# Attention into a routed expert layer: row stores on GpSimd's queue, loads first in a step, logits two steps after sums, and the early block split during attention

## The chip, the cores and the metric

The kernel runs on one core of a Trainium2 chip. A core has TensorE (PE, matmuls), VectorE (DVE), ScalarE (ACT), GpSimd (POOL) and SyncE (SP, which here only issues DMAs), each with an in-order queue of its own. The metric is the device time of one execution in microseconds; the figure shown is a median of several runs.

## What is computed

The reference is attention with a soft cap on the scores, whose output is fed to a layer of eight experts, one per token.

```python
# q, k, v: 8 batches x 12 heads x 448 tokens x 64
s = scale * (q @ k.T);  s = cap * tanh(s / cap)
a = exp(s - max);  x = (a / sum(a)) @ v            # rows x: 3584 tokens x 768
logits = x @ w_gate                                # 8 experts
e = argmax(logits);  g = softmax(logits)[e]
out[t] = g[t] * (relu(x[t] @ w1[e]) @ w2[e])       # w1: 768 x 1024, w2: 1024 x 768
```

Tokens are sorted by expert, and each expert's tokens are computed in blocks.

## The kernel before

**Attention.** A group of four heads (`m`, 24 of them, three to a batch) has seven tiles of 64 keys. A step `k` (84 of them, `STEPS`) handles two tiles: TensorE makes the scores of tiles 2k and 2k+1 (line 242), ScalarE applies two tanh (line 251) and, for the step before, one exp (line 254), TensorE multiplies the tiles of three steps before with the values (`pv`, line 300), and VectorE adds up the exponentials (`adds`, line 259). The scores have two PSUM buffers, the exponentials `pt` four, and one `m` at a time has its output in PSUM (`po`). So when the first tile of a step is the last of its `m`, the second tile's `pv` is held back to the next step, after `outp` (line 307) has copied the output to `ot`.

**What hangs on a batch.** When the last `m` of batch b is done (step n + 3 in the code), its work is put into the following steps from a table: `at(step, place, function)`, where the places within a step are `act`, `pe0` (before `pv`), `pe1` (after it) and `v` (after `adds`). `sums` makes the denominators, `logits` the gate's products, `rec_v` and `rec_p` the reciprocals, spread over partitions, `rec_c` (line 387) writes them into the last six columns of the row tile `yt`, `log_v` and `log_p` finish the logits, `route_v`, `route_s` and `route_g` find the expert and its weight, `place_p` and `place_v` the slot of each token, `place_d` scatters token numbers to the slots by indirect DMAs of GpSimd (line 503). `turn` (line 318) transposes each output into `yt`, and `store` (line 469) sends a batch's rows, 448 x 4 pieces of 792 bytes, to DRAM in four quarters. The casts of `rec_v` are on GpSimd in all batches but the last.

**SP's queue.** It carries the loads of q, k and v (lines 173 to 176, for the `m` two ahead, issued at the end of a step once the scores of an `m` are done, two buffers), the stores, and, in the second half, `values_load` of the chosen expert's row and the sixteen weight loads of the early block (line 776). All of these are issued in program order, and each waits at the head of the queue until it may go.

**The early block.** After four of eight batches the expert with the most tokens is chosen (`first_block`), and 224 of its tokens, block -2, are gathered (`load_x`, indirect DMAs of GpSimd), scaled (`scale_x`, four steps before the end), transposed by `trans_x` (line 880) and split into a high and a low part by `split_x` (lines 886, 887), so that three matmuls with a shorter type stand for one in float32. The weights are split likewise (`high` on ScalarE, line 791; `low` on VectorE or GpSimd, line 796). In the kernel before, the transposes and splits of block -2 start when the last scores are done, together with the last steps of attention.

**After attention.** TensorE's program order is: `sums` and `logits` of the last batch, `up(-2, 0)` (line 906, 18 matmuls), `up(-2, 1)`, `rec_p`, `up(-2, 2)`, `up(-2, 3)`, `log_p`, and so on, with the last batch's routing threaded between the work of block -2. Block -1, and then the large and small blocks, follow from about 400 us to the end.

The lines around the loop that the change rearranges:

```python
        if not live:
            if k == STEPS:
                split_w1(0, G)
                split_xs(-2, 0, 2)
                split_w1(1, G)
        do(k, "pe0")
```

Of the kernel before, what the change touches and what calls it, by code (L numbers as in the profile page):

```python
# [125 lines left out]
def attention_moe(tc, qT, kT, vL, capd, wgL, w1a, w1b, w2a, w2b, cst, cmk, out):  # L126
# [14 lines left out]
    rpool = pools("rpool", side="right")  # L141
    raw = pools("raw", bufs=2, side="right")
# [9 lines left out]
    raws = {}  # L152

    def load(m, part):

        b, i = divmod(m, NQ)
        p = slice(2 * i, 2 * i + 2)
        if part == 0:
            qr = raw.tile([128, 2, S], F32, name="qr")
            kr = raw.tile([128, 2, S], F32, name="kr")  # L160
            raws[m] = qr, kr, pb.tile([128, KT, 2, D], F32, name="vr", bufs=3)
        qr, kr, vr = raws[m]
        if m == 0:
            if part == 0:
                nc.sync.dma_start(out=kr[:, :, 0:128], in_=kT[b, :, p, 0:128])
                nc.scalar.dma_start(out=qr[:, 0], in_=qT[b, :, 0])
                nc.sync.dma_start(out=qr[:, 1], in_=qT[b, :, 1])
                nc.scalar.dma_start(out=capt, in_=capd)
                nc.sync.dma_start(out=kr[:, :, 128:S], in_=kT[b, :, p, 128:S])
            else:  # L170
                nc.sync.dma_start(out=vr, in_=vL[b, :, i])
        elif part == 0:
            nc.sync.dma_start(out=kr, in_=kT[b, :, p])
            nc.sync.dma_start(out=qr, in_=qT[b, :, p])
        else:
            nc.sync.dma_start(out=vr, in_=vL[b, :, i])
# [85 lines left out]
    def adds(k):  # L262

        t = 2 * k
        m, g = divmod(t, KT)
        pt = pts[k]
        if m % 2 == 0 and g == 0 or m % 2 == 1 and g == 1:
            accs[m] = pb.tile([128, 2, 2, S], F32, name="acc")
            p4s[m] = pb.tile([128, 2, S], F32, name="p4", bufs=4)
        if g == KT - 1:  # L270

            p4 = p4s[m]
            add(p4, accs[m][:, 0], accs[m][:, 1])
            add(p4, p4, pt[:, 0])
        elif m % 2 == 0:
            if g == 2:
                add(accs[m], pts[k - 1], pt)
            elif g == 4:
                add(accs[m], accs[m], pt)
        elif g == 1:  # L280
            add(accs[m][:, 0], pts[k - 1][:, 1], pt[:, 0])
        elif g == 3:
            add(accs[m][:, 1], pts[k - 1][:, 1], pt[:, 1])
            add(accs[m][:, 0], accs[m][:, 0], pt[:, 0])
        else:
            add(accs[m], accs[m], pt)
            add(p4s[m], accs[m][:, 0], accs[m][:, 1])
# [178 lines left out]
    def store(b, quarters=range(4)):  # L466
        xv = xd[4 * b * S : 4 * (b + 1) * S, :].rearrange("(q j a) x -> a j q x", j=32, a=4)
        for a in quarters:
            nc.sync.dma_start(out=xv[a], in_=yts[b][32 * a : 32 * a + 32])
# [49 lines left out]
    def first_block():  # L519
# [10 lines left out]
        for i in range(2):  # L530
# [10 lines left out]
        row = nc.values_load(  # L541
            ti[0:1, 0:1],
# [5 lines left out]
        f0.update(e0=e0, oh=oh, t=t, ti=ti, row=row)  # L548
# [240 lines left out]
    def high(i, f):  # L789
        w, r = ((w1s, w1r), (w2s, w2r))[i - 1]  # L790
        A.copy(out=w[f][0], in_=r[f // 4][:, f % 4, :])
# [6 lines left out]
    def split_w1(f, e=V):  # L798
        high(1, f)
        low(1, f, e)  # L800
# [55 lines left out]
    m = {}  # L856
# [25 lines left out]
    def split_x(j, k, e):  # L882
# [3 lines left out]
        A.copy(out=xh, in_=xt)  # L886
# [105 lines left out]
    for b in range(B - 1):  # L992

        n = (KT * (b * NQ + NQ) - 1) // 2
        at(n + 3, "pe1", sums, b)
        at(n + 4, "pe0", logits, b)
        at(n + 4, "v", turn, b * NP + 4)
        at(n + 4, "v", rec_v, b, G)
        at(n + 5, "v", turn, b * NP + 5)
        at(n + 5, "v", log_v, b)  # L1000
        at(n + 6, "pe1", rec_p, b)
        at(n + 6, "pe1", log_p, b)
        at(n + 7, "v", rec_c, b)
        at(n + 7, "v", route_v, b)
        at(n + 7, "v", store, b, range(0, 2))
        at(n + 8, "act", route_s, b)
        at(n + 8, "pe1", place_p, b)
        at(n + 8, "v", store, b, range(2, 4))
        at(n + 8, "v", route_g, b)
        at(n + 9, "v", place_v, b)  # L1010
        for q in range(4):
            at(n + 10 + q // 2, "v", place_d, b, q)
# [6 lines left out]
    n_first = (KT * B_FIRST * NQ - 1) // 2 + 10  # L1019
    at(0, "v", constants)  # L1020
    at(n_first, "v", first_block)
    for i in range(2 * FC):
        at(n_first + 1 + i + i // 2, "v", load_w0, i)
# [4 lines left out]
    at(STEPS - 4, "v", scale_x, -2)  # L1028

    held = []  # L1030
    for k in range(STEPS + 3):
        live = k < STEPS
        if live:
# [6 lines left out]
        if not live:  # L1040
            if k == STEPS:
                split_w1(0, G)
                split_xs(-2, 0, 2)
                split_w1(1, G)
        do(k, "pe0")
# [13 lines left out]
        if k == STEPS + 1:  # L1059
            split_xs(-2, 2)  # L1060
        do(k, "v")
        for n in range(QUADS - 2):
            if k == (KT * (n + 1) - 1) // 2 + 1:
                load(n + 2, 0)
                load(n + 2, 1)
        if k == STEPS - 1:
            pools.close("raw")
            xp = m["xp"] = pools("xp", side="right", **tw)
            for i in "hl":
                m["x" + i] = xp.tile([128, KC, LARGE], F32R, name="x" + i)  # L1070
            for f in range(2):
                w1s[f] = chunk(xp, f"w1{f}")
            for i in range(XT):
                trans_x(-2, i)
# [11 lines left out]
    b = B - 1  # L1086
    sums(b)
    logits(b)
# [4 lines left out]
    up(-2, 0)  # L1093
# [21 lines left out]
    store(b)  # L1115
# [221 lines left out]
```

## Time and profile before

| | us |
|---|---|
| median of 3 runs | 884.2 (883.1 to 886.51) |
| profiled execution | 883.69 |
| its span, first to last instruction | 881.9 |
| TensorE busy | 813.8 (92%) |
| VectorE busy | 552.4 (63%) |
| ScalarE busy | 473.3 (54%) |
| GpSimd busy | 358.0 (41%) |

Attention takes the span to about 340 us; from 444 us on TensorE hardly pauses. TensorE's matmuls overlap and their ends are modelled, so its busy share is not its load. A group's row gives line, engine, operation, what is written from what, the count, then busy us and mean ns, then the engine's idle time just before and what ended most of it. A row of waits gives the engine and line that waited, for whom, us in total, times, and the longest. A row of the timeline gives start, duration, engine, line, operation, count, and in brackets the idle time before it. SPq is SP's queue of DMA issues.

### The profile page before, as it was taken

To read this page: it belongs to the slowest core of one execution; us is meant where nothing else is said; L and a number is where in the kernel's file an instruction comes from. 1 tells how busy PE (TensorE), PEld (TensorE's weight loads), DVE (VectorE), ACT (ScalarE), POOL (GpSimd) and SP (SyncE) were. 2 spreads that over 40 slices of the span, in tenths; PEclk is the share of its full clock that TensorE was granted. 3 is DMA by queue.
4 is the path that set the end of the run, shared out by engine and by line. 5 is a ranking of instruction groups with operands and counts; after the bars stand their busy time and mean duration, and the time that the engine had idled before them with its cause. 6 is when DMAs were issued, how large, how long until landed. Compare 5 with 4: busy or idle time off the path is not lost. (4 is left out here: it accounts for less than half of the span.)

```text
span 881.9 us, 14403 instructions
## 1 busy us (share of the span) xinstructions
PE 813.8 (92%) x5716; PEld 586.1 (66%) x5716; DVE 552.4 (63%) x944; ACT 473.3 (54%) x556; POOL 358.0 (41%) x333
## 2 busy tenths in 40 slices
PE   8998989897979797798999999999999999999894
PEld 3223333332323333598899999999999999999793
DVE  2677787778667869965664944836638448366620
ACT  7988988897879888332443432423323324234310
POOL 1002120212142203555747067477475673745610
PEclk9999999998999999898999999999999999999997
DMA  6316161618395812042474112451721124444200
GB/s 220 126 64 190 64 191 63 192 67 214 127 237 175 262 64 66 1 98 92 155 302 154 66 38 72 168 201 65 287 87 42 42 73 177 192 172 170 67 34 34
DMA packets 44955, 112.67 MB, mean 128 GB/s; under 512 B 8321, under 2 KB 27203, under 8 KB 41808
## 3 DMA queue, kind: packets, MB, share of 16 engines
q1 hardware_dynamic: 28496, 51.16, 19.3%
q0 software_dynamic: 16096, 60.28, 19.2%
q8 instruction: 47, 0.77, 0.4%
q10 hardware_dynamic: 288, 0.23, 0.1%
q14 instruction: 28, 0.23, 0.1%
HBM read 101.77 MB, written 23.04 MB: 142 GB/s over the span
## 5 line engine op out<-in xcount | busy, mean ns | idle before, releaser
L910 ACT ACTIVATE hb<-ph 128x448 fp32r<-128x448 f32 (+1 forms) x80 | 38.4, 481 | 284.2 <-PE ph L906 279.2
L251 ACT ACTIVATE pt<-sp,qsc 128x896 f32<-128x896 f32 x168 | 161.0, 1015 | 46.0 <-PE po L300 25.2
L242 PE MATMUL sp<-qr,kr 64*64 64x448 f32 x1344 | 152.7, 560 | 26.0 <-DMA qr<-in_qT 21.8
L911 DVE SCALAR_TENSOR_TENSOR hb<-ph,hb 128x448 fp32r<-128x448 f32 (+1 forms) x80 | 43.1, 541 | 186.5 <-ACT hb L910 186.4
L300 PE MATMUL po<-pt,vr 64*64 64x448 f32 x1344 | 149.1, 559 | 3.1 <-DVE ot L307 3.1
L751 POOL DMA_INDIRECT xg<-xd,xi x114 | 129.7, 1138 | 54.7 <-issue 32.6
L254 ACT ACTIVATE pt<-pt,capt 128x1792 f32<-128x1792 f32 x84 | 151.2, 1802 | 0.0
L242 PEld LDWEIGHTS sp<-qr,kr 64*64 64x64 f32 x1344 | 46.2, 135 | 112.4 <-ACT pt L251 55.1
L300 PEld LDWEIGHTS po<-pt,vr 64*64 64x64 f32 x1344 | 57.0, 139 | 82.0 <-issue 75.4
L761 POOL DMA_INDIRECT out<-ys,xi x84 | 90.6, 1078 | 25.6 <-issue 23.2
L503 POOL DMA_INDIRECT ids<-tokg,slots x32 | 38.8, 1214 | 129.8 <-DVE slots L497 122.5
L259 DVE TENSOR_TENSOR acc<-acc,pt 128x1792 f32<-128x1792 f32 (+1 forms) x36 | 61.2, 1700 | 37.9 <-ACT pt L254 37.9
L259 DVE TENSOR_TENSOR acc<-pt 128x896 f32<-128x896 f32 (+1 forms) x36 | 50.2, 1396 | 15.6 <-ACT pt L254 15.5
L370 POOL CAST rb<-rec 96x56 bf16<-96x56 f32 x7 | 6.4, 918 | 130.6 <-DVE rec L362 130.6
L886 ACT CAST xh<-xt 128x448 fp32r<-128x448 f32 (+1 forms) x60 | 28.5, 504 | 40.6 <-DVE xt L880 40.6
L751 POOL DMA_INDIRECT w1r<-in_w1b,widx x8 | 11.1, 1386 | 84.5 <-DVE w17l L796 83.9
L307 DVE COPY ot<-po 128x448 f32<-128x448 f32 x48 | 27.5, 614 | 23.2 <-PE po L300 23.2
L880 DVE STREAM_TRANSPOSE xt<-xg 128x448 f32<-128x448 f32 (+1 forms) x60 | 31.5, 550 | 1.0
L887 DVE TENSOR_TENSOR xl<-xt,xh 128x448 fp32r<-128x448 f32 (+1 forms) x57 | 31.2, 573 | 0.7 <-ACT xh L886 0.5
L870 DVE TENSOR_TENSOR xg<-xg,sc 128x448 f32<-128x448 f32 (+2 forms) x60 | 27.9, 535 | 0.3
L259 DVE TENSOR_TENSOR p<-acc 128x896 f32<-128x896 f32 x24 | 25.8, 1077 | 0.4
L906 PE MATMUL ph<-xl,w10h 128*128 128x448 f32 (+1 forms) x60 | 21.5, 358 | 3.3 <-DVE xl L887 3.1
(353 smaller groups left out, 1922.4 us busy)
## 6 DMA issues: line engine op xcount, KB each, us to landing
vr<-in_vL SPq DMA_DIRECT2D x24, 448.0 KB, 5.8
kr<-in_kT SPq DMA_DIRECT2D x23, 448.0 KB, 5.3
qr<-in_qT SPq DMA_DIRECT2D x23, 448.0 KB, 5.8
xd<-yt SPq DMA_DIRECT2D x20, 346.5 KB, 6.0
xd<-w2r SPq DMA_DIRECT2D x12, 346.5 KB, 6.3
xg<-xd,xi POOLq DMA_INDIRECT x114, 2.7
w1r<-in_w1a SPq DMA_DIRECT2D x4, 384.0 KB, 9.0
w1r<-in_w1b SPq DMA_DIRECT2D x4, 384.0 KB, 6.2
```

What stands on the lines that cost most here:

```text
L242: PE.matmul(sp[w, r, 0:S], kr[h, c, 64 * g : 64 * g + 64], qr[h, c, :], start=True, stop=True)
L251: A.activation(out=pts[t // 2][:, t % 2], in_=sps.pop(t)[:, :, 0:S], func=AF.Tanh, scale=qsc)
L254: A.activation(out=pts[k], in_=pts[k], func=AF.Exp, scale=capt)
L259: V.tensor_tensor(out=o, in0=a, in1=b, op=ALU.add)
L300: PE.matmul(pvs[m][c][w, 0:S], vr[r, g, j, :], pt[r, j, :], start=g == 0, stop=g == KT - 1)
L503: i = G.indirect_dma_start(out=ids, out_offset=bass.IndirectOffsetOnAxis(ap=slots[0:p, c : c + 1].bitcast(U32), axis=0), in_=tokg[0:p, c, ...
L751: G.indirect_dma_start(out=dst, out_offset=None, in_=src, in_offset=bass.IndirectOffsetOnAxis(ap=idx.bitcast(U32), axis=0), bounds_check=b ...
L761: i = G.indirect_dma_start(out=dst, out_offset=bass.IndirectOffsetOnAxis(ap=idx.bitcast(U32), axis=0), in_=src, in_offset=None, bounds_che ...
L880: V.transpose(out=xt.rearrange("p (q j) -> p q j", j=32), in_=xg[:, 0 : n // 32, 32 * k : 32 * k + 32])
L887: e.tensor_tensor(out=m["xl"][:, k, 0:n], in0=xt, in1=xh, op=ALU.subtract)
L910: A.activation(out=hh, in_=ph, func=AF.Relu)
L911: V.scalar_tensor_tensor(out=hl, in0=ph, scalar=0.0, in1=hh, op0=ALU.max, op1=ALU.subtract)
```

## The change

- `store` takes the issuing engine: GpSimd for the first seven batches, all four quarters together one step after `rec_c`, SP for the last.
- The loads of q, k and v are issued at the start of a step, ahead of its scores, and no longer after its `v` work.
- `logits` moves from before `pv` in step n + 4 to after `pv` in step n + 5; all that follows it (`log_v`, `rec_p`, `log_p`, `rec_c`, the routing, `place_*`) comes one step later. `rec_v` goes ahead of `turn`. The choice of the early block and its weight loads come one to three steps later, and `values_load` stands on its own, two steps after the choice.
- `scale_x` of block -2 moves from four steps before the end to eleven; its six transposes and splits go into steps 75 to 82, two at a time, the copies and the subtractions on GpSimd. The first two weight chunks are split on GpSimd alone, in step 83. The buffers for the rows are held from the start.
- The last `fold` (the sum of two halves of the exponentials) is taken after the loop; `up(-2, 0)` is ahead of the last batch's `logits` and `sums`, which change places.

```diff
-            add(p4s[m], accs[m][:, 0], accs[m][:, 1])
+            if m < QUADS - 1:
+                fold(m)
+
+    def fold(m):
+        add(p4s[m], accs[m][:, 0], accs[m][:, 1])
...
-    def store(b, quarters=range(4)):
+    def store(b, e):
...
-        for a in quarters:
-            nc.sync.dma_start(out=xv[a], in_=yts[b][32 * a : 32 * a + 32])
+        for a in range(4):
+            e.dma_start(out=xv[a], in_=yts[b][32 * a : 32 * a + 32])
...
-    def split_x(j, k, e):
+    def split_x(j, k, e, eh=A):
...
-        A.copy(out=xh, in_=xt)
+        (eh.copy if eh is A else eh.tensor_copy)(out=xh, in_=xt)
...
+        d = n + 5
         at(n + 3, "pe1", sums, b)
-        at(n + 4, "pe0", logits, b)
+        at(n + 4, "v", rec_v, b, G)
         at(n + 4, "v", turn, b * NP + 4)
-        at(n + 4, "v", rec_v, b, G)
         at(n + 5, "v", turn, b * NP + 5)
-        at(n + 5, "v", log_v, b)
-        at(n + 6, "pe1", rec_p, b)
-        at(n + 6, "pe1", log_p, b)
-        at(n + 7, "v", rec_c, b)
-        at(n + 7, "v", route_v, b)
-        at(n + 7, "v", store, b, range(0, 2))
-        at(n + 8, "act", route_s, b)
-        at(n + 8, "pe1", place_p, b)
-        at(n + 8, "v", store, b, range(2, 4))
-        at(n + 8, "v", route_g, b)
-        at(n + 9, "v", place_v, b)
+        at(d, "pe1", logits, b)
+        at(d + 1, "v", log_v, b)
+        at(d + 2, "pe1", rec_p, b)
+        at(d + 2, "pe1", log_p, b)
+        at(d + 3, "v", rec_c, b)
+        at(d + 3, "v", route_v, b)
+        at(d + 4, "act", route_s, b)
+        at(d + 4, "pe1", place_p, b)
+        at(d + 4, "v", store, b, G)
+        at(d + 4, "v", route_g, b)
+        at(d + 5, "v", place_v, b)
         for q in range(4):
-            at(n + 10 + q // 2, "v", place_d, b, q)
+            at(d + 6 + q // 2, "v", place_d, b, q)
...
-    n_first = (KT * B_FIRST * NQ - 1) // 2 + 10
+    n_first = (KT * B_FIRST * NQ - 1) // 2 + 11
     at(0, "v", constants)
     at(n_first, "v", first_block)
+    at(n_first + 2, "v", first_row)
     for i in range(2 * FC):
-        at(n_first + 1 + i + i // 2, "v", load_w0, i)
+        at(n_first + 3 + i + i // 2, "v", load_w0, i)
...
-    at(STEPS - 4, "v", scale_x, -2)
+    at(STEPS - 11, "v", scale_x, -2)
+    for k in range(KC):
+        at(STEPS - 9 + k // 2 * 3, "v", trans_x, -2, k)
+        at(STEPS - 8 + k // 2 * 3, "v", split_x, -2, k, G, G)
...
     for k in range(STEPS + 3):
         live = k < STEPS
+        for n in range(QUADS - 2):
+            if k == (KT * (n + 1) - 1) // 2 + 1:
+                load(n + 2, 0)
+                load(n + 2, 1)
...
-            if k == STEPS:
-                split_w1(0, G)
-                split_xs(-2, 0, 2)
-                split_w1(1, G)
-        do(k, "pe0")
...
-        if k == STEPS + 1:
-            split_xs(-2, 2)
         do(k, "v")
-        for n in range(QUADS - 2):
-            if k == (KT * (n + 1) - 1) // 2 + 1:
-                load(n + 2, 0)
-                load(n + 2, 1)
         if k == STEPS - 1:
             pools.close("raw")
-            xp = m["xp"] = pools("xp", side="right", **tw)
...
+            wa = pools("wa", side="right", **tw)
             for f in range(2):
-                w1s[f] = chunk(xp, f"w1{f}")
-            for i in range(XT):
-                trans_x(-2, i)
+                w1s[f] = chunk(wa, f"w1{f}")
+            for f in range(2):
+                split_w1(f, G, G)
+    fold(QUADS - 1)
...
+    up(-2, 0)
+    logits(b)
     sums(b)
-    logits(b)
...
-    up(-2, 0)
```

More of the change, by code (lines that the diff above doesn't have):

```diff
@@ L141, in attention_moe @@
     rpool = pools("rpool", side="right")
+    xp = pools("xp", side="right")
     raw = pools("raw", bufs=2, side="right")
@@ L152, in attention_moe, with load @@
     raws = {}
-    def load(m, part):
-        b, i = divmod(m, NQ)
+    m = {"xp": xp}
+    for i in "hl":
+        m["x" + i] = xp.tile([128, KC, LARGE], F32R, name="x" + i)
+    def load(mq, part):
+        b, i = divmod(mq, NQ)
         p = slice(2 * i, 2 * i + 2)
@@ L160, in load @@
             kr = raw.tile([128, 2, S], F32, name="kr")
-            raws[m] = qr, kr, pb.tile([128, KT, 2, D], F32, name="vr", bufs=3)
-        qr, kr, vr = raws[m]
-        if m == 0:
+            raws[mq] = qr, kr, pb.tile([128, KT, 2, D], F32, name="vr", bufs=3)
+        qr, kr, vr = raws[mq]
+        if mq == 0:
             if part == 0:
@@ L540, in first_block, with first_row @@
         V.tensor_copy(out=ti, in_=t)
-        row = nc.values_load(
-            ti[0:1, 0:1],
+        f0.update(e0=e0, oh=oh, t=t, ti=ti)
+    def first_row():
+        f0["row"] = nc.values_load(
+            f0["ti"][0:1, 0:1],
             engines=[mybir.EngineType.SP],
@@ L547, in first_block @@
         )
-        f0.update(e0=e0, oh=oh, t=t, ti=ti, row=row)
     def second_block():
@@ L787, in chunk, with high @@
         return [pool.tile([128, DM], F32R, name=name + i) for i in "hl"]
-    def high(i, f):
+    def high(i, f, e=A):
         w, r = ((w1s, w1r), (w2s, w2r))[i - 1]
-        A.copy(out=w[f][0], in_=r[f // 4][:, f % 4, :])
+        (e.copy if e is A else e.tensor_copy)(out=w[f][0], in_=r[f // 4][:, f % 4, :])
     def low(i, f, e=V):
@@ L796, in low, with split_w1 @@
         e.tensor_tensor(out=lo, in0=r[f // 4][:, f % 4, :], in1=hi, op=ALU.subtract)
-    def split_w1(f, e=V):
-        high(1, f)
+    def split_w1(f, e=V, eh=A):
+        high(1, f, eh)
         low(1, f, e)
@@ L854, in load_x @@
             gather(xg[:, g, :], xd[0:rows, :], xi[:, g : g + 1], rows - 1)
-    m = {}
     def scale_x(j):
@@ L1039, in attention_moe @@
             expo(k - 1)
-        if not live:
-            if k == STEPS:
-                split_w1(0, G)
-                split_xs(-2, 0, 2)
-                split_w1(1, G)
-        do(k, "pe0")
         last = None
@@ L1058, in attention_moe @@
             adds(k - 2)
-        if k == STEPS + 1:
-            split_xs(-2, 2)
         do(k, "v")
-        for n in range(QUADS - 2):
-            if k == (KT * (n + 1) - 1) // 2 + 1:
-                load(n + 2, 0)
-                load(n + 2, 1)
         if k == STEPS - 1:
             pools.close("raw")
-            xp = m["xp"] = pools("xp", side="right", **tw)
-            for i in "hl":
-                m["x" + i] = xp.tile([128, KC, LARGE], F32R, name="x" + i)
+            wa = pools("wa", side="right", **tw)
             for f in range(2):
-                w1s[f] = chunk(xp, f"w1{f}")
-            for i in range(XT):
-                trans_x(-2, i)
+                w1s[f] = chunk(wa, f"w1{f}")
+            for f in range(2):
+                split_w1(f, G, G)
+    fold(QUADS - 1)
     pools.close("ps_s", "pb")
@@ L1114, in attention_moe @@
     rec_c(b)
-    store(b)
+    store(b, nc.sync)
     pools.close("op")
```

## The prediction

> **What bounds the kernel now.** First the stretches, engine by engine (us, then busy us of PE, PEld, DVE, ACT, POOL, the granted TensorE clock, the DMA share and GB/s).
>
> ```profile
> 15.00:340.00 325.00, 293.06 (x2852) 108.39 (x2844) 240.42 (x383) 282.60 (x248) 56.09 (x67) 0.96 0.50 147
> 340.00:361.00 21.00, 11.89 (x88) 4.76 (x80) 20.08 (x34) 11.29 (x16) 10.70 (x8) 0.84 0.01 1
> 444.00:862.00 418.00, 413.99 (x2170) 386.99 (x2169) 233.29 (x374) 142.39 (x232) 233.27 (x207) 1.00 0.34 124
> ```
>
> From 444 to 862 TensorE is busy 414 of 418 us and no edit touches it. The change acts on attention (to 340) and the passage from attention to the experts (340 to 361), where TensorE works 11.9 of 21 us at clock 0.84. In attention a step is two tanh and one exp on ScalarE against 16 score and 16 PV matmuls. The timelines give the pace of each side:
>
> ```profile
> 40.18 1.93 ACT L251 ACTIVATE pt<-sp,qsc 128x896 f32<-128x896 f32 x2
> 43.65 1.94 ACT L251 ACTIVATE pt<-sp,qsc 128x896 f32<-128x896 f32 x2
> ...
> 41.27 1.88 PE L242 MATMUL sp<-qr,kr 64*64 64x448 f32 x16
> ...
> 99.90 1.68 PE L242 MATMUL sp<-qr,kr 64*64 64x448 f32 x16
> 102.91 1.68 PE L242 MATMUL sp<-qr,kr 64*64 64x448 f32 x16
> ```
>
> ScalarE needs 43.65 - 40.18 = 3.47 us a step. TensorE, when it is behind, needs 102.91 - 99.90 = 3.01. So ScalarE bounds an undisturbed step, and TensorE regains 0.46 us a step. How far may it fall behind unseen? The scores that begin at 41.27 feed the tanh at 43.65; starved, tanh follows its scores by 1.00 (99.90, then 100.90 below). The slack is 43.65 - 41.27 - 1.00 = 1.38 us. The waits and the page's group of the tanh say where it is used up:
>
> ```profile
> PE sp L242 <- DMA qr<-in_qT: 21.8, 6, 4.8
> ...
> L251 ACT ACTIVATE pt<-sp,qsc 128x896 f32<-128x896 f32 x168 | 161.0, 1015 | 46.0 <-PE po L300 25.2
> ```
>
> ScalarE idles 46.0 us before tanh. Its timeline sorts this by what went before (the rest, 4.3, is the start): the first and last of nine gaps after a late load (together 25.1), of four after a batch that ends on the first tile of a step ("even": 2.55, 2.84, 2.84, 2.84, together 11.1), of three after the other batches ("odd", 3.7), of four small ones (1.8).
>
> ```profile
> 85.53 1.91 ACT L251 ACTIVATE pt<-sp,qsc 128x896 f32<-128x896 f32 x2 [3.60 <-PE po L300]
> 305.29 1.01 ACT L251 ACTIVATE pt<-sp,qsc 128x896 f32<-128x896 f32 x1 [1.27 <-PE sp L242]
> ...
> 56.76 1.91 ACT L251 ACTIVATE pt<-sp,qsc 128x896 f32<-128x896 f32 x2 [2.55 <-PE po L300]
> 318.66 1.01 ACT L251 ACTIVATE pt<-sp,qsc 128x896 f32<-128x896 f32 x1 [2.84 <-PE po L300]
> ...
> 100.90 1.01 ACT L251 ACTIVATE pt<-sp,qsc 128x896 f32<-128x896 f32 x1 [1.22 <-PE sp L242]
> 276.54 1.91 ACT L251 ACTIVATE pt<-sp,qsc 128x896 f32<-128x896 f32 x2 [1.22 <-PE sp L242]
> ...
> 67.74 1.01 ACT L251 ACTIVATE pt<-sp,qsc 128x896 f32<-128x896 f32 x1 [0.46 <-PE sp L242]
> 329.64 1.01 ACT L251 ACTIVATE pt<-sp,qsc 128x896 f32<-128x896 f32 x1 [0.46 <-PE sp L242]
> ```
>
> **Part 1, stores off SP's queue, loads first: -25.1, and 4.4 come back.** SP's queue and TensorE's timeline around the first late load:
>
> ```profile
> SPq L469 <- DVE w2r L387: 54.9, 3, 18.4
> ...
> 69.52 4.28 SPq L469 DMA_DIRECT2D xd<-w2r  x4
> 73.89 1.62 SPq L173 DMA_DIRECT2D kr<-in_kT  x1
> 75.56 1.59 SPq L174 DMA_DIRECT2D qr<-in_qT  x1
> ...
> 81.79 2.21 PE L242 MATMUL sp<-qr,kr 64*64 64x448 f32 x16 [3.22 <-DMA qr<-in_qT]
> ```
>
> SP stands at the store for up to 18.4 us until VectorE's rec_c (L387) has written the last columns, and the loads issued at 73.89 and 75.56 were stuck behind it. It is used 81.79 - 75.56 = 6.2 us after its issue; a buffer comes free 3.5 steps = 12.1 us before its next use, so without the wait some 5 us are spare. The nine gaps go. What is late next: a group of heads (m) ends in the stretch after each batch's routing, and its output must be copied by VectorE before the next PV may start, and VectorE has its burst there:
>
> ```profile
> 331.16 0.51 DVE L387 COPY yt<-ms 64x84 f32<-64x84 f32 x2
> 333.55 0.38 DVE L444 TENSOR_REDUCE ob<-ohm 128x32 bf16<-128x128 f32 x1
> ```
>
> rec_c and route_v take 333.93 - 331.16 = 2.8 us beside an average load of 240.4 / 325 x 3.47 = 2.6 a step: 5.4 against 3.47, so VectorE is 1.9 late, and the late load has hidden that so far. Against the slack of 1.38 it costs 0.5; I take 0.63 a batch, for the smaller burst that follows it, 4.4 in seven. Bounds: 0, and 1.8 a batch or 12 (no slack left). The move of first_row and load_w0 by three steps costs nothing: the weights are used only after 340.
>
> The store itself, four quarters of 448 rows of 792 bytes, now occupies POOL. No plain DMA on POOL is in this trace; the nearest row moves 128 rows (min/median/max ns):
>
> ```profile
> L503 POOL DMA_INDIRECT ids<-tokg,slots x32: 907/1000/2797, 79.3 to 401.0; - x32
> ```
>
> Lower bound 1.0 us a quarter (a price per instruction), upper 3.5 (a price per row). I take 2.0, 8 us a batch. POOL is busy 56.1 of 325 us, so this lies beside other work, but POOL is in order: behind the store stand the next place_d, load_x and, from step 73, the splits. What waits for those comes in part 3.
>
> **Part 2, logits two steps after sums: -7.8; log_p: -0.8.**
>
> ```profile
> 54.08 1.70 PE L339 MATMUL ms<-ot,wg 128*32 128x448 f32 x12
> 55.71 2.49 PE L300 MATMUL po<-pt,vr 64*64 64x448 f32 x24
> ```
>
> Logits takes 55.71 - 54.08 = 1.63, and sums has the same 12 matmuls. In an even batch the PV of a held tile, whose pt buffer the next tanh needs, stands behind logits. With logits gone from there the gap falls by 1.63, four times: 6.5. At its new place TensorE is some 0.2 behind and loses 3.01 + 1.63 - 3.47 = 1.17 in the step: 1.4 against a slack of 1.38, free. In an odd batch sums leaves TensorE 1.4 behind, one step regains 0.46, logits adds 1.17: 2.1 - 1.38 = 0.7 to 0.8 remain of 1.22, so 1.3 for three. Together 7.8; bounds 3.6 (the lag is never regained) and 11. The log_p gaps of 0.46 shrink since rec_v and log_v now have a turn less in front: 0.8 of 1.8; bounds 0 and 1.8.
>
> **Part 3, the passage to the experts: -5.** TensorE and VectorE there (the row at 841.41 is from the chain that ended last):
>
> ```profile
> 343.56 6.01 PE L300 MATMUL po<-pt,vr 64*64 64x448 f32 x56 [3.09 <-DVE ot L307]
> 356.47 2.45 PE L325 MATMUL ms<-p,cs 128*32 128x448 f32 x7 [6.02 <-DVE p L259]
> 361.03 0.39 PE L906 MATMUL ph<-xh,w10h 128*128 128x256 f32 x1
> ...
> 841.41 2.15 PE ph L906 x18
> ...
> 346.56 1.85 DVE L887 TENSOR_TENSOR xl<-xt,xh 128x256 fp32r<-128x256 f32 x1 [0.52 <-ACT xh L886]
> 355.32 1.09 DVE L259 TENSOR_TENSOR p<-acc 128x896 f32<-128x896 f32 x1
> 357.15 1.05 DVE L887 TENSOR_TENSOR xl<-xt,xh 128x256 fp32r<-128x256 f32 x3
> 359.72 0.63 DVE L359 STREAM_TRANSPOSE st<-ms 96x448 f32<-96x448 f32 x1
> 364.50 0.19 DVE L370 CAST rb<-rest 96x56 bf16<-96x56 f32 x1
> ```
>
> PV ends at 349.57; up(-2,0) starts 11.5 us later. VectorE's last fold comes at 355.32, behind transposes and subtractions of the rows. These move into attention (the transposes on VectorE, the copies and subtractions on POOL), as scale_x moves from four steps before the end to eleven. Then up(-2,0), 18 matmuls in 2.2 us, fills the hole to 351.8; fold falls to about 353, with some blocking by POOL; logits runs ahead of sums, which ends at 355.4 (two blocks of 1.63 after 351.8, and 0.3 of waiting); up(-2,1) ends at 357.6. Before, it ended at 361.03 + 2 x 2.2 = 365.4: 7.8 gained. But rec_v needs 364.69 - 359.72 = 5.0 after sums, and only one up, no longer two, covers it: 2.8 are lost, 5 remain. Everything after hangs on that chain or on TensorE's own queue, and shifts with it. The 3.09 at 343.56 stays: VectorE loses scale_x ahead of it and gains transposes and place_v.
>
> What it rests on is POOL:
>
> ```profile
> L887 POOL TENSOR_TENSOR xl<-xt,xh 128x256 fp32r<-128x256 f32 x3 | 2.2, 746 | 1.9 <-ACT xh L886 1.9
> 346.31 1.82 POOL L796 TENSOR_TENSOR w10l<-w1r,w10h 128x768 fp32r<-128x768 f32 x1 [0.42 <-ACT w10h L791]
> L226 POOL MEMSET xg<- 128x2772 f32 x1 | 2.4, 2408 | 0.3 <-POOLq L1326 0.3
> ```
>
> A cast on POOL costs at least the memset's 0.87 ns an element (0.67 us for 768) and at most the two-input 1.82; I take 1.2, and 0.5 for 256. The last store follows rec_c, now one step later, at 331.16 + 3.47 = 334.6. Then 8.0 of store, two x splits of 1.25, and w1(0) of 3.0: 348.1, before PV ends. With 3.5 a quarter it is 354.1, and up(-2,0) is 4.5 late. Beside the row at 346.31, VectorE's subtraction at 346.56 took 1.85, where three of its kind took 1.05 at 357.15: POOL's splits block VectorE's adds, some 2 us in the last ten steps, which is why fold is at 353 and not 351. Bounds of the part: -8 (no wait for rec_v) and +4 (everything late and VectorE blocked before the last PV). The Trainium skill, GPSIMD Engine Reference, section Engine selection, says that one-input work on POOL runs at about line rate, two-input work at half of VectorE's; by that the cast is at the lower bound and w1(0) done 0.5 earlier, which changes nothing.
>
> **The sum.** The profiled execution took 883.7 (span 881.9): 883.7 - 25.1 + 4.4 - 7.8 - 0.8 - 5.0 = 849.4. The median is 884.2, 0.5 above it, so 850.
>
> **Rivals.**
> - *Slow issue on POOL* (3.5 a quarter). For it: rows, not bytes, are what POOL handles. Against: nothing in the row of 1000 ns separates the two. Part 3 goes from -5 to +2, a rec_v behind a store adds 2: 859. Chance 0.14.
> - *VectorE takes over the late loads' place.* For it: 240.4 busy of 325 now, in about 290 afterwards 83%, in bursts. Against: it caused one TensorE wait of note, 3.09. At 12 instead of 4.4: 858. Chance 0.11.
> - *Loads stay late*, by bandwidth and not by the queue, so that the change doesn't do what it says. For it: the DMA share of 0.50 rises with the shorter attention, and weights come in its second half. Against: the 6.2 from issue to use. Half of the 14.8 of the last three batches' gaps stays: 857 (0.07); all 25 stay: 871 (0.04).
> - *POOL becomes the bound: slower.* Per batch POOL would have four quarters, four place_d of 1.0 and more, some 5 in all, and the casts of rec_v, 1 or 2, in a period of about 38.6 us (10.5 steps and the remaining gaps); from 8 us a quarter on, rec_v of the next batch waits behind the store and every microsecond costs 4 a batch, 28 in all. At 10 us: 850 + 56 = 906; it decides against the change from 9.2. Against it: the longest of 32 issues is 2.8, the median 1.0. Chance 0.05. The Trainium skill, SBUF — State Buffer, section Who interferes with whom, tells of a DMA issued from POOL that a VectorE copy stretched five times, because POOL could not write its descriptors; five times my 2.0 is this rival. The row's 2.8 against 1.0 shows stretching, but of few.
> - Two or three of the first three together: 875 to 890, chance 0.04, half of it no change, half slower.
>
> **How the numbers follow.** The forecast has 0.55. It alone spans 840 to 857; to leave out no more than 2 in 10 the range goes to 868, taking in the first two rivals and half of the third, and to 838 for the favourable bounds. A change under 0.5% (4.4 us) can't be told from none. Faster: 0.55 + 0.14 + 0.11 + 0.11 = 0.91, taken as 0.90; same 0.03; slower 0.07.
>
> **What would show it.** The DMA wait of 21.8 gone and the granted clock of attention at 1.00; the even gaps near 1.1; store issues on POOL near 2 us; up(-2,0) right after the last PV. Wrong: gaps of ScalarE released by VectorE's output copies, POOL's splits ending after PV, or kr and qr landing later than 12 us after issue.

## The result, and the profile after

| | before | after |
|---|---|---|
| median, us | 885.36 (883.1 to 886.8) | 850.46 (849.67 to 851.36) |
| profiled execution, us | 883.69 | 850.79 |
| its span, us | 881.9 | 848.9 |

The ratio is 0.9608, 95% interval 0.9582 to 0.9634: 3.9% faster, and 0.5 us from the 850 predicted. That the sum came out so close is in part luck: the passage to the experts gave nothing where 5 us were expected, the late loads' part gave more than expected, and 2.6 us came from a place that the sum did not have. So the time alone says little about the working.

The experiments ran in three groups; in the second and third (all but e1 to e4) the chip granted half clock for stretches of 14 us and more, from some point between 388 and 424 us on, whatever the kernel (the kernel before took 954 and 939 us there), so those kernels are compared by the stages ahead of that and not by their totals.

The stretches of the profile after, first of 15 to 310 us, then of the passage, divided where its clock changes (us, then busy us of PE, PEld, DVE, ACT, POOL, the granted clock, the DMA share, GB/s):

```profile
15.00:310.00 295.00, 287.24 (x2852) 103.56 (x2844) 243.93 (x387) 284.68 (x251) 104.29 (x106) 1.00 0.58 160
...
318.46:327.97 9.51, 8.71 (x60) 5.26 (x60) 8.06 (x10) 4.25 (x6) 8.59 (x6) 1.00 0.02 3
328.00:331.38 3.38, 0.04 (x1) 0.00 (x0) 3.38 (x1) 1.83 (x3) 3.38 (x3) 1.00 0.00 0
331.38:341.62 10.24, 4.99 (x29) 4.79 (x30) 8.66 (x19) 0.03 (x1) 4.03 (x3) 0.50 0.00 0
```

In attention the clock is 1.00 (0.96 before). In the passage there are 3.38 us in which TensorE only ends a matmul and VectorE is at one instruction, and then 10.24 us at half clock. The page's groups of attention, and of the stores that GpSimd now issues:

```profile
L255 ACT ACTIVATE pt<-sp,qsc 128x896 f32<-128x896 f32 x168 | 161.0, 1019 | 14.0 <-PE sp L246 6.0
...
L477 POOL DMA_DIRECT2D xd<-yt x16 | 10.6, 669 | 31.4 <-DVE yt L395 30.5
```

ScalarE's idle time before tanh fell from 46.0 to 14.0 us, by 32.0; the span fell by 33.0. ScalarE's timeline shows what is left, one batch of each kind, and the largest gap that VectorE makes:

```profile
55.09 1.91 ACT L255 ACTIVATE pt<-sp,qsc 128x896 f32<-128x896 f32 x2 [0.75 <-PE po L308]
69.73 1.91 ACT L255 ACTIVATE pt<-sp,qsc 128x896 f32<-128x896 f32 x2 [0.53 <-DVE acc L263]
80.65 1.91 ACT L255 ACTIVATE pt<-sp,qsc 128x896 f32<-128x896 f32 x2 [0.20 <-DVE pos L496]
...
98.99 1.91 ACT L255 ACTIVATE pt<-sp,qsc 128x896 f32<-128x896 f32 x2 [0.75 <-PE sp L246]
106.55 1.91 ACT L255 ACTIVATE pt<-sp,qsc 128x896 f32<-128x896 f32 x2 [0.50 <-PE po L308]
...
234.91 1.91 ACT L255 ACTIVATE pt<-sp,qsc 128x896 f32<-128x896 f32 x2 [0.81 <-DVE pos L496]
```

The gaps after an even batch are 0.75 us, those after an odd one 0.75, those at log_p 0.50 to 0.54. Where the late loads of three batches stood, 0.20, 0.20 and 0.81 are left. No gap of a late load is left, and the wait for qr does not appear among the waits.

Three marks divide the run: the first tanh of step 3, the end of the last PV, and the first matmul of block -1. Before, the tanh starts at 15.60 and block -1 at 400.01; after:

```profile
15.73 1.91 ACT L255 ACTIVATE pt<-sp,qsc 128x896 f32<-128x896 f32 x2
```

```profile
311.17 4.28 PE L308 MATMUL po<-pt,vr 64*64 64x448 f32 x24 [2.55 <-DVE ot L315]
314.53 3.92 PE L308 MATMUL po<-pt,vr 64*64 64x448 f32 x38
318.38 0.39 PE L915 MATMUL ph<-xh,w10h 128*128 128x256 f32 x1
...
336.13 0.23 PE L388 MATMUL ms<-rb,mk 96*128 96x56 bf16 x1 [8.10 <-DVE rb L378]
...
369.60 0.39 PE L915 MATMUL ph<-xh,w10h 128*128 128x256 f32 x1
...
409.05 0.62 PE L946 MATMUL y<-w27h,hb 128*128 128x384 f32 x2 [1.00 <-DVE hb L920]
```

and in the kernel before:

```profile
440.69 0.62 PE L937 MATMUL y<-w27h,hb 128*128 128x384 f32 x2 [1.99 <-DVE hb L911]
```

The last PV ends at 318.45 (314.53 + 3.92); 349.57 before. Counted from the tanh of step 3, that is 31.3 us earlier. But from there to block -1 it takes 369.60 - 318.45 = 51.15 us, and before 400.01 - 349.57 = 50.44: **the passage, from which 5 us were expected, gave nothing.** up(-2,0) does start right at the end of PV, as intended; then `rec_p` (the row at 336.13) waits 8.10 us. From the tanh of step 3 to block -1 the change gains 384.41 - 353.87 = 30.5 us, and from there to the end 2.6 more that were not predicted; 1.0 of these is TensorE's hole ahead of `w27` of block -1, now 1.00 us and 1.99 before, the rest was not traced to a place.

A single trace leaves some doubt in such differences. e2, e6, e7, e8 and e11 below have the same instructions as the kernel after up to the last PV, but for e2's loads. PV ends 301.4 to 301.5 us after the tanh of step 3 in four of them, 303.1 in e8 and 302.7 in the kernel after; in these two a stretch of half clock (after: 310.90 to 314.31) fell on the last PV. At block -1 e2 stands at 353.50 and the kernel after at 353.87. So differences under about half a microsecond at block -1 are not told from none.

### The profile page after: what moved, and what is told of

It is laid out like the page before. It is cut to its first block, busy times and chain, and to the rows that moved or that the text cites. A ratio compares the mean times of both kernels' runs of the same rounds, so it can differ in the third digit from the quotient of the medians.

```text
span 848.9 us, 14416 instructions
## 1 busy us (share of the span) xinstructions
PE 806.6 (95%) x5716; PEld 579.5 (68%) x5716; DVE 554.6 (65%) x938; ACT 469.7 (55%) x548; POOL 412.9 (49%) x375
## 5 line engine op out<-in xcount | busy, mean ns | idle before, releaser
L246 PE MATMUL sp<-qr,kr 64*64 64x448 f32 x1344 | 150.9, 550 | 6.0 <-ACT pt L255 4.7
L308 PE MATMUL po<-pt,vr 64*64 64x448 f32 x1344 | 145.8, 541 | 2.5 <-DVE ot L315 2.5
L246 PEld LDWEIGHTS sp<-qr,kr 64*64 64x64 f32 x1344 | 42.2, 132 | 96.5 <-ACT pt L255 69.8
L511 POOL DMA_INDIRECT ids<-tokg,slots x32 | 48.5, 1515 | 47.1 <-DVE slots L505 39.4
L378 POOL CAST rb<-rec 96x56 bf16<-96x56 f32 x7 | 1.6, 228 | 90.6 <-DVE rec L370 90.6
L895 ACT CAST xh<-xt 128x448 fp32r<-128x448 f32 (+1 forms) x54 | 26.1, 513 | 31.2 <-DVE xt L889 31.2
L896 DVE TENSOR_TENSOR xl<-xt,xh 128x448 fp32r<-128x448 f32 (+1 forms) x51 | 26.3, 541 | 0.2 <-issue 0.2
L477 POOL DMA_DIRECT2D xd<-yt x16 | 10.6, 669 | 31.4 <-DVE yt L395 30.5
```

What stands on the lines that cost most here:

```text
L246: PE.matmul(sp[w, r, 0:S], kr[h, c, 64 * g : 64 * g + 64], qr[h, c, :], start=True, stop=True)
L308: PE.matmul(pvs[m][c][w, 0:S], vr[r, g, j, :], pt[r, j, :], start=g == 0, stop=g == KT - 1)
L511: i = G.indirect_dma_start(out=ids, out_offset=bass.IndirectOffsetOnAxis(ap=slots[0:p, c : c + 1].bitcast(U32), axis=0), in_=tokg[0:p, c, ...
```

## Experiments: which half of part 1 does the work

Line numbers are those of the kernel after. In the first group the kernel before took 882.64 us.

**e1_store_sp**: SP's queue issues the stores again, behind the loads.

```diff
-        at(d + 4, "v", store, b, G)
+        at(d + 4, "v", store, b, nc.sync)
```

> The changed kernel with the first seven stores issued by SP again, at the same place in the program (one step after rec_c, with the loads still first in a step). Theory A, the order of the two on SP's queue decides: the load that comes due in the step before the store is now ahead of it, so no load is late; 850 to 854 us, no wait of TensorE for qr above 1 us in total. Rival B, the queue itself decides (four quarters of 1.07 us and the loads' own slowed issue): most of the 21.8 us of waits come back, 865 to 873 us. Rival C, GpSimd's queue costs something that SP's does not: 845 to 849 us.

**e2_loads_last**: the loads at the end of a step again; GpSimd keeps the stores.

```diff
         live = k < STEPS
-        for n in range(QUADS - 2):
-            if k == (KT * (n + 1) - 1) // 2 + 1:
-                load(n + 2, 0)
-                load(n + 2, 1)
...
         do(k, "v")
+        for n in range(QUADS - 2):
+            if k == (KT * (n + 1) - 1) // 2 + 1:
+                load(n + 2, 0)
+                load(n + 2, 1)
```

> The changed kernel with the loads at the end of a step again, stores still on GpSimd. Theory A and rival B agree: with no store on SP's queue the place within the step doesn't matter, 850 to 852 us. If loads-first gives something by itself (weight loads of the early block standing ahead of a q, k, v load), 853 to 858 us.

**e3_store_sp_first**: SP issues all four quarters right behind `rec_c`, and the loads are at the end of a step, as in e2.

```diff
         at(d + 3, "v", route_v, b)
+        at(d + 3, "v", store, b, nc.sync)
...
-        at(d + 4, "v", store, b, G)
```

> The changed kernel with both halves of part 1 undone: stores by SP, in the step of rec_c, and loads at the end of a step, so that the store is ahead of a load again as in the kernel before. Theory A and rival B: the late loads return, six waits of 2 to 5 us for qr, 868 to 876 us, and the granted clock of attention below 1.00. If late loads came from bandwidth and not from the queue: 850 to 855 us.

Measured: e1 854.03 (ratio to before 0.9667, 0.9635 to 0.9699), e2 851.03 (0.9638, 0.9606 to 0.9670), e3 899.8 (1.0188, 1.0153 to 1.0224). In e1 and e2 attention, from the tanh of step 3 to that of step 83, takes 292.15 and 292.21 us, after 292.22: either half of part 1 alone removes every late load. e3, with neither, is slower than the kernel before, and than the 868 to 876 expected. SP's queue in e1 and in e3, and TensorE's wait in e3:

```profile
65.63 0.33 SPq L177 DMA_DIRECT2D kr<-in_kT  x1
66.05 0.38 SPq L178 DMA_DIRECT2D qr<-in_qT  x1
72.77 4.27 SPq L477 DMA_DIRECT2D xd<-w2r  x4
```

```profile
72.76 4.27 SPq L477 DMA_DIRECT2D xd<-w2r  x4
77.13 1.62 SPq L177 DMA_DIRECT2D kr<-in_kT  x1
78.80 1.79 SPq L178 DMA_DIRECT2D qr<-in_qT  x1
```

```profile
85.51 3.26 PE L246 MATMUL sp<-qr,kr 64*64 64x448 f32 x16 [7.50 <-DMA qr<-in_qT]
```

The store takes 4.27 us on SP's queue in both. In e1 it hinders nobody, since the load has gone at 65.63; in e3 the same load goes at 77.13 and each of its two issues takes 1.6 to 1.8 us, where 0.33 and 0.38 is usual. So the order in the queue decides, not the engine. That e3 came out above its range is due to `rec_c`, which the change has put a step later: in e3 the store starts 7.2 us after the scores that free the load's buffer (65.57), in the kernel before 1.9 us after them (67.67). The six waits for qr add up to 41.1 us, where the kernel before had 21.8. What e1 loses against e2 (3.0 us) lies behind the last PV, and is taken up below.

**e9_part1_undone**: both halves taken back, two quarters behind `rec_c` and two a step later.

```diff
+        at(d + 3, "v", store, b, nc.sync, range(0, 2))
...
-        at(d + 4, "v", store, b, G)
+        at(d + 4, "v", store, b, nc.sync, range(2, 4))
```

The loads are again as in e2.

> The changed kernel with its first part alone undone, as near as it goes: the stores are on SyncE's queue again, two quarters right behind rec_c and two a step later, and the loads stand at the end of a step; logits and the early block stay where the change put them. rec_c is one step later than before, so the load stands behind two quarters of the same step, no longer behind four. The prediction gave the part 25.1 less the 4.4 that come back, 20.7: 871. What attention gained in the changed kernel's trace (32.4) less what the run with the logits put back lost (3.8) leaves 26 to 29: 876 to 879. The run with all four quarters ahead of the load (899.8, six waits up to 8.5) less two quarters of some 1.1 us at each of six loads leaves 887. Waits of TensorE for qr of 20 us or more together in each case.

Measured by stages: attention takes 316.49 us, 24.3 more than after, with TensorE waiting for qr again:

```profile
PE sp L246 <- DMA qr<-in_qT: 17.5, 5, 4.3
```

From the tanh of step 3 to block -1 it takes 380.69 us against 353.87, 26.8 more. That agrees with the 26 to 29 that the other two parts leave over, not with the 20.7 of the prediction nor with what e3 would give; the 24.3 of attention alone lie between the first two. The qr waits, at 17.5, came out under the 20 expected.

## Experiment: part 2 alone

**e4_logits_adjacent**: `logits` is ahead of `pv` in step n + 4 again; what follows it stays a step later.

```diff
-        at(d, "pe1", logits, b)
+        at(n + 4, "pe0", logits, b)
```

> The changed kernel with logits ahead of PV in the step after sums again; log_v and all behind it stay one step later than in the kernel before. By the prediction's ledger 6.5 us come back in the four even batches (gaps of 0.94 grow to about 2.6) and about 1 in the three odd ones: 856 to 859 us. Rival: the time moves into the later steps' lag and only 2 to 3 us come back, 852 to 854 us.

Measured 854.58 (0.9678, 0.9644 to 0.9711), 3.6 above e2 on the same chip, less than the 856 to 859 of the prediction's ledger and a little more than the rival's 852 to 854; attention takes 295.99 us, 3.8 more than after. ScalarE's timeline of e4, one batch of each kind:

```profile
57.52 1.90 ACT L255 ACTIVATE pt<-sp,qsc 128x896 f32<-128x896 f32 x2 [2.55 <-PE po L308]
82.29 1.91 ACT L255 ACTIVATE pt<-sp,qsc 128x896 f32<-128x896 f32 x2 [0.18 <-PE po L308]
97.62 1.90 ACT L255 ACTIVATE pt<-sp,qsc 128x896 f32<-128x896 f32 x2 [1.22 <-PE sp L246]
```

With logits at its old place the even gap is 2.55 and the odd one 1.22, as before the change; moving it saves 1.80 four times and 0.47 three times, 8.6 us, a little over the 7.8 of the prediction. But the move has a price two steps later, at log_p. There the kernel after has gaps of 0.53 or 0.54 us four times, where e4 has none, and of 0.50 three times, where e4 has 0.18: 3.1 us. Where the late loads were it has 1.2 us and e4 0.6. 8.6 less 3.1 less 0.6 is 4.9, and by that ScalarE's idle time differs; 3.8 was measured, and the 1.1 between them are not accounted for. The even gap at log_p (69.73 above) ended with VectorE's addition:

```profile
64.37 1.16 DVE L315 COPY ot<-po 128x448 f32<-128x448 f32 x2 [1.93 <-PE po L308]
67.63 2.01 DVE L263 TENSOR_TENSOR acc<-pt 128x1792 f32<-128x1792 f32 x1
```

The addition ends at 69.64. It stands behind the output copy, which waited for TensorE's PV, and behind the three operations of `log_v` between the two rows; the odd gap ended with PV itself. So TensorE is not free of the logits' time within the batch: part of it comes up two steps later, in the even batches by way of VectorE.

## Experiments: where the gain of part 3 went

VectorE and GpSimd of the kernel after in the passage:

```profile
325.73 0.65 DVE L367 STREAM_TRANSPOSE st<-ms 96x448 f32<-96x448 f32 x1 [1.45 <-PE ms L333]
326.30 9.14 DVE L563 TENSOR_TENSOR cnt<-base,kc 128x8 f32<-128x8 f32 x1
335.37 0.49 DVE L370 RECIPROCAL rec<-st 96x56 f32<-96x56 f32 x1
```

```profile
324.77 1.85 POOL L806 TENSOR_TENSOR w12l<-w1r,w12h 128x768 fp32r<-128x768 f32 x1
326.55 1.85 POOL L806 TENSOR_TENSOR w13l<-w1r,w13h 128x768 fp32r<-128x768 f32 x1
...
333.62 1.79 POOL L806 TENSOR_TENSOR w16l<-w1r,w16h 128x768 fp32r<-128x768 f32 x1
```

An addition of 8 columns took 9.14 us. It ended at 335.44, and the last of six subtractions of weights on GpSimd, which ran without a pause from 324.77 ("the row"), at 335.41. That an operation of VectorE ends only with GpSimd's is called the lock below. The kernel before has the same addition and the same six subtractions, and its timeline has:

```profile
360.28 0.12 DVE L553 TENSOR_TENSOR cnt<-base,kc 128x8 f32<-128x8 f32 x1
```
The 9.14 us stand ahead of `rec_v`, whose first reciprocal is the third row, and so are most of `rec_p`'s 8.10.

**e5_passage_undone**: part 3 alone taken back.

```diff
-    at(STEPS - 11, "v", scale_x, -2)
-    for k in range(KC):
-        at(STEPS - 9 + k // 2 * 3, "v", trans_x, -2, k)
-        at(STEPS - 8 + k // 2 * 3, "v", split_x, -2, k, G, G)
+    at(STEPS - 4, "v", scale_x, -2)
...
+        if k == STEPS:
+            split_w1(0, G)
+            split_xs(-2, 0, 2)
+            split_w1(1, G)
...
-            for f in range(2):
-                split_w1(f, G, G)
-    fold(QUADS - 1)
+            for i in range(XT):
+                trans_x(-2, i)
...
-    up(-2, 0)
-    logits(b)
     sums(b)
+    logits(b)
...
+    up(-2, 0)
```

> The changed kernel with its third part alone undone: the rows of the early block are scaled four steps before the end and transposed and split after the last scores, the last fold stands with the additions, sums and logits of the last batch stand ahead of up(-2,0). As the prediction priced it, the part was worth 5.0, so 855 to 856 us. My theory after the changed kernel's trace: up(-2,0) did fill the hole, but the wait of rec_p took 8.1 us in its place, because VectorE's first small two-input operation of the filler was held up behind GpSimd's row of weight subtractions; so the part is worth only 1 to 2 us, 851 to 853, with TensorE's hole of some 6 us ahead of sums back and the wait of rec_p under 2 us. Attention itself (the tanh of step 3 to that of step 83) 292 to 293 us, as in the changed kernel.

Measured: attention 294.25 us, 2.0 more, and at block -1 354.00 us against 353.87. TensorE's hole of 7.00 us ahead of sums is back, and there is no wait at `rec_p`:

```profile
307.72 0.19 PE L480 MATMUL ms<-ob,mk 128*128 128x40 bf16 x1 [2.48 <-DVE ob L448]
...
326.58 2.45 PE L329 MATMUL ms<-p,cs 128*32 128x448 f32 x7 [7.00 <-DVE p L263]
```

So in this kernel **part 3 is worth 0.1 us**, which is not told from nothing: it exchanges one hole for another.

**e6_lows_on_dve** (run again as **e11_lows_again**): five of the six subtractions go to VectorE.

```diff
-    for f in range(2, 5):
-        split_w1(f, G)
-    split_w2(0, G)
+    for f in range(2, 4):
+        split_w1(f)
+    high(1, 4)
+    high(2, 0)
...
     log_v(b)
     fill(100)
+    low(1, 4)
+    low(2, 0)
...
-    low(1, 5, G)
+    low(1, 5)
```

> The changed kernel, with the low parts of five weight chunks after attention computed by VectorE, in two places of the passage, where GpSimd computed them in one unbroken row. Theory of the lock (VectorE's two-input operation gets SBUF only where GpSimd pauses): the 9.14 us of the 128x8 operation falls under 2 us, the wait of rec_p from 8.1 to under 1.5, the half clock after it is gone too, and the time falls by 6 to 8 us, to 842 to 844. Rival, that the operation waits for something of its own or that VectorE is simply full there: the wait of rec_p stays over 5 us and the time is 848 to 854, since VectorE has some 5 us more work.

> The kernel with five low parts on VectorE once more, now beside the next three. At the first matmul of block -1 it stood 5.8 us ahead of the changed kernel, and 7.0 at that block's fifth chunk: 843.5 to 845. Rival, that the gain is given back between there and the end: 848 to 851.

Measured: block -1 starts 348.04 and 348.02 us after the tanh of step 3, 5.8 ahead of the kernel after both times. VectorE of e6:

```profile
328.66 0.12 DVE L563 TENSOR_TENSOR cnt<-base,kc 128x8 f32<-128x8 f32 x1
328.77 0.50 DVE L370 RECIPROCAL rec<-st 96x56 f32<-96x56 f32 x1
...
330.35 0.95 DVE L806 TENSOR_TENSOR w12l<-w1r,w12h 128x768 fp32r<-128x768 f32 x1
```

The addition takes 0.12 us, and `rec_p` has no wait above 0.3. A subtraction takes VectorE 0.95 us, GpSimd 1.8. Of the 8.10 us 2.35 come back: up(-2,4) waits that long for an evacuation that now stands behind two of the subtractions. In e11 TensorE's clock is 0.50 from 323.63 to 327.04, and from there to block -1 it is 1.00. The totals expected (842 to 845) could not be measured.

**e7_filler_late**: the filler, of which the 128x8 addition is the first operation, begins after `rec_v`.

```diff
-    filler.append(second_block())
     rec_v(b, V)
+    filler.append(second_block())
```

> The changed kernel, with the filler (the small counts of the second block) begun only after rec_v on VectorE; nothing else moved, and GpSimd's subtractions as they were. If GpSimd's row locks out whichever two-input operation of VectorE comes first, the subtraction within rec_v takes the stretch over, the wait of rec_p stays at 6 to 9 us and the time at 849 to 852. If the 128x8 operation itself was late (for its own input), rec_v goes through, the wait falls under 2 us and the time to 842 to 845.

Measured: the wait at `rec_p` is 5.84 us (6.42 in e2, which has the filler where the kernel after has it), block -1 starts at 352.95, 0.9 earlier than after and 0.5 earlier than in e2. VectorE:

```profile
328.06 0.50 DVE L370 RECIPROCAL rec<-st 96x56 f32<-96x56 f32 x1
328.60 6.87 DVE L378 CAST rb<-rec 96x56 bf16<-96x56 f32 x1
335.50 0.21 DVE L380 TENSOR_TENSOR rest<-rec,rb 96x56 f32<-96x56 f32 x1
```

The lock stays and hits another operation; the transpose and the reciprocal ahead of it passed. I expected the subtraction of `rec_v` to be hit; it was the cast ahead of it (0.19 us elsewhere in the same kernel), which reads one operand only. It too ends with GpSimd's row, at 335.47 against 333.61 + 1.81 = 335.42; the reciprocal, started during the row, was not held up. So the addition was not late for something of its own.

The same explains what e1 loses: there GpSimd is free of stores, begins its row earlier, and the victim is the last `fold`, which sums waits for.

```profile
323.42 6.84 DVE L263 TENSOR_TENSOR p<-acc 128x896 f32<-128x896 f32 x1
```

TensorE waits 5.60 us for it at 330.31. In e9 it waits 5.62 us at the same place; that is why e9 loses 26.8 at block -1 and 24.3 in attention.

**e12_undone_lows**: e5 with the five subtractions on VectorE, as in e6. It asks what part 3 would be worth without the lock.

```diff
-    for f in range(2, 5):
-        split_w1(f, G)
+    for f in range(2, 4):
+        split_w1(f)
     up(-2, 0)
-    split_w2(0, G)
+    high(1, 4)
+    high(2, 0)
...
+    low(1, 4)
+    low(2, 0)
...
-    low(1, 5, G)
+    low(1, 5)
```

> The kernel with the third part undone, and with the same five low parts on VectorE. If GpSimd's row of subtractions took what the third part would have given, then without that row the part is worth 5 to 6 us, and this kernel takes 848.5 to 850.5 beside 843.5 to 845 of the one that keeps the part. If the third part is worth nothing in any case (something later than it sets the time), both take the same within 1 us.

Measured: block -1 starts 354.91 us after the tanh of step 3, 6.9 behind e11, which keeps part 3. Of these, 5.9 lie between the last PV and block -1, where the prediction had 5.0, and 1.0 ahead of it. So part 3 is worth 6.9 us as soon as GpSimd's row is gone, and 0.1 with it. Its mechanism is sound; its gain was taken on the way. The totals, 921.85 and 915.49, point the same way, but single runs of the two overlap.

**e8_both**: e6, with `low(1, 6)` and all splits of block -1's rows on VectorE as well.

```diff
-    low(1, 6, G)
+    low(1, 6)
...
-        split_xs(-1, k, k + 1, V if k < XT else G)
+        split_xs(-1, k, k + 1, V)
```

> As the kernel with the five low parts on VectorE, one more of the weights' low parts on VectorE, and the splits of the rows of block -1 on VectorE alone, where GpSimd had half of them. If the 2.58 us that TensorE waits for the rows of block -1 at 374 are of the same kind (VectorE held up by GpSimd's two-input work), another 1 to 3 us fall away, 840 to 842. If VectorE becomes the bound there, the gaps ahead of the first matmuls of block -1 grow and it is 844 to 850.

Measured: block -1 starts at 347.87, 0.2 ahead of e6; its fifth weight chunk starts at 366.86 against 367.89, where the kernel after stands at 374.87. That is one us of the 1 to 3 expected.

**e10_better**: e8 with `route_g` a step later, two subtractions moved behind the evacuation of up(-2,2), and a third behind up(-2,3). The diff is against e8.

```diff
-        at(d + 4, "v", route_g, b)
+        at(d + 5, "v", route_g, b)
...
-    low(1, 4)
-    low(2, 0)
...
     up(-2, 2)
-    low(1, 5)
+    low(1, 4)
+    low(2, 0)
     up(-2, 3)
+    low(1, 5)
```

> The kernel with six low parts and all splits of block -1 on VectorE, and two more edits: route_g one step later, behind the output copy of step 83 on VectorE (TensorE waited 2.55 us for that copy), and two low parts behind the evacuation of up(-2,2) (TensorE waited 1.71 us for it). The stages of the kernel without these two give 850.5 less 6.0 to 8.0, 842.5 to 844.5; the two edits together 1.5 to 2.5 more: 840 to 843. If route_g is late for the scatter of token numbers, or VectorE's order only moves the waits on, 843 to 846.

Measured: the waits that it aims at shrink, and another grows:

```profile
309.25 6.01 PE L308 MATMUL po<-pt,vr 64*64 64x448 f32 x56 [1.34 <-DVE ot L315]
322.00 2.45 PE L347 MATMUL ms<-ot,wg 128*32 128x448 f32 x7 [3.53 <-DVE ot L315]
```

The last PV ends 299.66 us after the tanh of step 3 (302.72 after the change), but logits then waits 3.53 us for the last output copy, and block -1 starts at 347.85, as in e8; its fifth chunk, at 367.95, is 1.1 behind e8. The 1.5 to 2.5 us expected of the two moves did not come: moving VectorE's work only moved the wait. e6, e8 and e10 reach block -1 some 6 us ahead of the kernel after; what they take in all on an undisturbed chip is not measured.

## Why the prediction was right, step by step

| from the tanh of step 3, us earlier at block -1 | predicted | undone alone |
|---|---|---|
| part 1: stores and loads | 25.1 - 4.4 = 20.7 | 26.8 (24.3 in attention) |
| part 2: logits and log_p | 7.8 + 0.8 = 8.6 | 3.2 (3.8 in attention) |
| part 3: passage | 5.0 | 0.1 |
| together | 34.3 | 30.1; measured 30.5 |

Behind block -1 another 2.6 us came that the sum did not have. That 30.1 comes so near 30.5 is partly luck: 3.4 of the 26.8 of e9 lie in the passage, where GpSimd's row holds up the last `fold`, which it does not in the kernel before. In attention alone the three runs give 24.3 + 3.8 + 2.0 = 30.1 of the 32.4 gained.

- **The late loads (25.1): right in mechanism and size.** e3 and e9 show the store ahead of the load as the cause. One detail was put too broadly: SP's stand of 18.4 us for rec_c is not the delay. Of it, only the 1.9 us count that lie behind the end of the scores that free the load's buffer (67.67 to 69.52); the store's own 4.28 us of issue and the slowed issues behind it (3.2 us for two, where 0.7 is usual) add more. e1's store waits for rec_c as well and costs attention nothing.
- **The 4.4 that come back: mis-sized.** The gaps at VectorE's copies are 0.20, 0.20 and 0.81, together 1.2, and none in the other batches. The term was 0.63 a batch; but for the 0.81 it is 0 or 0.20, near the lower bound.
- **Logits (7.8): right at its old place, wrong about the new one.** The even gaps fell by 1.8 to 2.1, more than the 1.63 claimed, to 0.75 where I said 1.1; by e4 the move accounts for 1.8 of it. "Free" for the new place was the failed step. The four gaps at log_p, expected to shrink from 1.8 by 0.8, make 2.1, and three of 0.50 stand after odd batches, where 0.18 stood before.
- **The passage (5.0): right up to rec_p, then wrong.** up(-2,0) fills the hole right behind the last PV, as said; sums ends 7.2 us after PV (5.8 said), up(-2,1) 9.6 (8.0 said). Then rec_p waits 8.10 instead of 2.8. I had seen that GpSimd's splits block VectorE (2 us in the last ten steps, a later fold), and had charged it only where the change adds work to GpSimd. The row that did it, `w12l` to `w16l`, is not new: before, it ran from 358.48, beside the same `rec_v` from 359.72. The 5.0 us that I took for `rec_v` itself held 2.7 us of the lock already: one addition took 1.25 us and one subtraction 1.74, which take 0.10 and 0.21 in e6. The failed step was to carry this 5.0 over as a fixed length. After the change VectorE did not get in between any two operations of the row, and from the end of sums to `rec_p` it took 10.4 us; why it got in before and not after stays open. The 3.09 ahead of the held tile stayed as 2.55, as said.
- **The store on GpSimd: below my lower bound.** 0.67 us a quarter where I took 2.0, between 1.0 and 3.5. GpSimd was no bound: w1(0) is split 4.0 us before PV ends, where 1.5 was said. That no GpSimd rival came true follows from this number.
- **The casts**: 0.83 us for 768 columns and mostly 0.40 for 256 (one took 1.21); taken were 1.2 and 0.5.
- The rivals "loads stay late" and "VectorE takes over" did not happen, nor did "slow issue" and "POOL becomes the bound", whose price for a store was not reached. The lock in the passage was none of them.

## What to carry to other kernels

A transfer that is late because of something ahead of it in its queue is cured by order; in e1 that did as much for attention as another engine's queue in e2. When work is moved so that a hole closes, look at what the other engines run at the new time, above all whether GpSimd has a row of two-input operations there; a total that comes out as forecast doesn't show it, and undoing one part at a time does. And a length read from the profile before, such as `rec_v`'s 5.0 us, may hold waits on another engine that change when the work moves. A hole filled ahead of a chain gains only as far as the chain itself moves.

## What was not expected of the hardware

- **GpSimd's row held VectorE for its whole length.** Six two-input operations of 1.8 us without a pause kept an 8-column addition for 9.14 us (e7: a cast for 6.87; e1: a fold, 1.07 us otherwise, for 6.84, over three operations; e3 and e9: the fold for 6.84 and 6.86; e2 and e4: the addition for 7.47 and 7.49). The Trainium skill, SBUF — State Buffer, section Who interferes with whom, says that VectorE and GpSimd share a pair of ports, that whoever issues first holds it for the whole of its instruction, and that casts can take it as well. A held cast agrees with that, but one instruction does not cover what after and these runs show. It does fit the kernel before and e5, whose rows of the same subtractions let VectorE in between any two. In e5:

```profile
330.99 1.23 DVE L561 TENSOR_TENSOR cnt<-cnt,fbo 128x8 f32<-128x8 f32 x1
332.14 0.18 DVE L374 CAST rb<-rec 96x56 bf16<-96x56 f32 x1
332.35 1.74 DVE L376 TENSOR_TENSOR rest<-rec,rb 96x56 f32<-96x56 f32 x1
```

```profile
328.60 1.81 POOL L802 TENSOR_TENSOR w12l<-w1r,w12h 128x768 fp32r<-128x768 f32 x1 [2.40 <-ACT w12h L797]
330.38 1.81 POOL L802 TENSOR_TENSOR w13l<-w1r,w13h 128x768 fp32r<-128x768 f32 x1
332.15 1.86 POOL L802 TENSOR_TENSOR w14l<-w1r,w14h 128x768 fp32r<-128x768 f32 x1
```

  There each waits for the end of one operation. What tells the two cases apart stays open. In after, e1 to e4, e7 and e9 the row follows GpSimd's own scatter DMAs at once, and in before and e5 it follows a pause for ScalarE's casts; no run varied that alone.
- **A store issued by GpSimd is cheap**: 0.67 us for a quarter of 448 pieces, where SP took 4.27 for four quarters. The DMA packets of the whole run fell at equal bytes; before and after:

```profile
DMA packets 44955, 112.67 MB, mean 128 GB/s; under 512 B 8321, under 2 KB 27203, under 8 KB 41808
```

```profile
DMA packets 34653, 112.69 MB, mean 133 GB/s; under 512 B 8321, under 2 KB 14659, under 8 KB 31504
```

- **TensorE's half clock around a wait of a few us**: the clock fell to half 3.3 us into the wait of 8.10 us and stayed there for 10.24 us, to 5.5 us behind the wait's end. There the matmuls of up(-2,2) start 0.21 us apart, where 0.12 is usual, so its 18 matmuls took 1.7 us more: the wait cost more than its length. The Trainium skill, TensorE: Matmul & The Clock Gate, Part 1, gives windows of about 3.4 us, after at least one of which idle the clock is halved; 10.24 is three times 3.41, which agrees in the size. It does not cover the wait of 2.55 us ahead of the held tile: the clock was 0.50 from 310.90 to 314.31, and TensorE worked until 308.62, within the 3.41 us ahead of that.
